# Hash attention with a gated MLP on one core: first-batch preparation in single steps, part of the later preparation moved into the first MLP layer, and a reordered start

## The chip, the cores and the metric

The kernel runs on one core of one Trainium2 chip. The metric is the device time of one execution in microseconds (us). A run on one core has no second core or die to be compared with, so runs are called slow only when they lie over 1.5% above the fastest of the same kernel. The profile's span is mostly some 1.8 us shorter than the device time of the same run.

In the profile's lines PE is TensorE's matmuls, PEld its weight loads, ACT is ScalarE, DVE VectorE, POOL GpSimd and SP SyncE; a q behind a name is that engine's instruction issue. A timeline line has the start and the length in us, the engine, the line of kernel.py, the operation, the tile written <- the tiles read, their sizes, a count, and in brackets the idle time before it and what ended that. A line of waits says who waited <- for whom: us in total, times, longest. Of the tiles, natq, natk and natv are loaded heads, n16x their 16-bit casts, blkq and blkk block transposes for the hash, projblk the projection, br the hash bits, qx and kx the extended queries and keys, and s_ps, av_ps and m_ps banks of PSUM.

## The reference, cut to what matters

```python
# q, k, v: (4, 8, 768, 64); proj: (64, 6)
q_bucket = sum over bits of ((q @ proj) > 0) * 2**bit        # 64 buckets
k_bucket = the same of k
scores = where(q_bucket == k_bucket, q @ k.T / 8, -1e9)
attn = softmax(scores)                                       # + 1e-9 in the denominator
x = (attn @ v) -> (3072, 512)
out = (h * cos(h)) @ w_out, h = x @ w_in                     # w_in 512x2048, w_out 2048x512
```

The kernel does the mask inside the score matmul: each query and key is extended by six rows of plus or minus a constant, its hash bits, so that a pair of unequal bits pushes the score far down before the exponential. Where no key matches, a uniform term of weight 1e-8 gives the mean of V.

## The kernel before

Heads are handled in pairs, two heads being 128 columns. Pair 0 to 15, four pairs for each of four batches. A *unit* is one key tile of one head: a score (two matmuls), one exponential of 128x768 on ACT, and, two units later, an AV tile of six matmuls. The preparation of a pair (casts on POOL, 32x32 block transposes on DVE, hash matmuls, bits, transposes of Q and K) is spread over the units of the pair before it. From the second batch on, every unit also takes one or two matmuls of the MLP's second layer of the batch before ("fill"); the first layer (L1, 16 pieces) stands in a block seven units into the next batch.

```python
    def hash_sums(pr, bank, cols, bh=None, t0=0):       # TensorE: 16 matmuls, four at a time
        nt = len(cols[0][2])
        hb = bank[:, 0:nt * 32]
        for c in range(2):
            for j, (w, hh, ts) in enumerate(cols):
                nc.tensor.matmul(out=hb[32 * j:32 * j + 32, :]..., lhsT=projblk[:, c]...,
                                 rhs=blk[pr][w][:, hh, ts[0]:ts[-1] + 1, c, :], ...)
        ...
    # ... cut: the start
        nc.scalar.dma_start(out=proj2, in_=proj.rearrange("(c p) i -> p c i", c=2))
        nc.sync.dma_start(out=nat[0][0][:, 0], in_=aps[0][:, 0])
        nc.scalar.dma_start(out=nat[0][1][:, 0], in_=aps[1][:, 0])
        ...
        warmup(8)                                       # matmuls of 512 columns on nothing
        for b_ in range(4):
            nc.vector.tensor_copy(
                out=projblk[32 * b_:32 * b_ + 32, :, b_, 0:NBITS], in_=proj2)
        blocks(0, 0)
    # ... cut: the preparation of the pairs, by unit
        for n in range(1, NP):
            s0 = 12 * (n - 1) - (0 if n < NEARLY else 4 if n == NEARLY else 6)
            if n < NEARLY:                              # pairs 1 to 4: transposes on TensorE
                at(s0 + 2, lambda n=n: load(n + 2, ...))
                at(s0 + o_, start)                      # casts, block transposes
                for half in range(2):
                    at(s0 + 3 + o_ + half, lambda ...: hash_a(half))
                at(s0 + 5 + o_, hash_b)
                ...
            else:                                       # pairs 5 to 15: transposes by DMA
                at(s0 - 1, lambda n=n: load(n + 1, nc.gpsimd))   # for 6 < n < 15
                at(s0, start)
                at(s0 + 2, hsh)                         # two DMA transposes into qx
                at(s0 + 3, hsh2)                        # hash, bits (DVE)
                at(s0 + 7, kc)                          # qx -> kx copies (DVE), bits by DMA
    # ... cut: the loop over units
            score(h, jt)
            pend.append((h, jt))
            for _ in range(2):
                if len(pend) > (4 if u < T else 2):
                    av_step()                           # the last tile of a head is followed by its norm (DVE)
            for f in acts.get(u, ()):
                f()
```

The softmax here doesn't subtract the row's maximum and nothing guards it: scores larger than these inputs give would overflow.

## Time and profile before

Median 310.24 us (310.15 to 310.26, three runs). The prediction shows the lines of this profile; in short:

| stage (us of the span) | length | what sets its pace |
|---|---|---|
| start, to the first exponential at 9.26 | 9.3 | loads, then one chain of hash, bits, transposes |
| first batch, to the first L1 matmul at 59.10 | 49.8 | ACT's 56 exponentials, with waits for scores |
| L1 of batch 0, rest of batch 1 and so on, to 263.2 | 204.1 | TensorE, 0.2 us idle in all |
| last MLP, to 308.4 | 45.2 | TensorE, then one copy and store |

The *pitch* of exponential n is its start minus that of exponential n-1 (there are 192; numbers are from 0); about 0.80 us when nothing is missing. "55 to 191" is the time from the start of the last exponential of the first batch to that of the last of all.

### The profile page before, as it was taken

What the parts mean: (1) busy time and instruction counts of PE and PEld (TensorE: products, weight loads), DVE (VectorE), ACT (ScalarE), POOL (GpSimd) and SP (SyncE); (2) the same over time, 40 slices, a digit from 0 to 9 for tenths busy, and PEclk for the clock granted to TensorE, in tenths of its full rate; (3) what the DMA queues carried; (4) which work ended last, traced back from release to release, by engine and by line L of the source; (5) the groups of instructions that cost most, each with busy time, mean ns of one, the idle gap of its engine ahead of it and who ended that gap; (6) DMA issues with size and microseconds to landing.
All of it is one profiled execution on the core that took longest, in us unless ns stands there. A gap on an engine that the chain in (4) does not pass through costs nothing.

```text
span 308.4 us, 7711 instructions
## 1 busy us (share of the span) xinstructions
PE 300.1 (97%) x3090; PEld 182.8 (59%) x3090; DVE 201.8 (65%) x434; ACT 234.3 (76%) x288; POOL 109.4 (35%) x180
## 2 busy tenths in 40 slices
PE   8899999899999999999999999999999999999995
PEld 3577677556566666555566666555566664565444
DVE  3665466877598988866777878766777343577211
ACT  3788999977899999766899999766899993577000
POOL 4898258378384684400064584100030000000000
PEclk9999999999999999999999999999999999999998
DMA  6969969289469856700169979200133223100121
GB/s 205 376 109 163 333 86 214 33 140 192 163 172 268 215 162 168 217 2 0 45 80 234 234 146 199 48 18 2 53 62 89 68 62 94 36 0 0 62 76 69
DMA packets 45332, 37.74 MB, mean 122 GB/s; under 512 B 32264, under 2 KB 39200, under 8 KB 45296
## 3 DMA queue, kind: packets, MB, share of 16 engines
q1 hardware_dynamic: 38080, 19.35, 28.9%
q0 software_dynamic: 6576, 17.17, 21.0%
q10 hardware_dynamic: 640, 0.72, 0.7%
q8 instruction: 24, 0.39, 0.5%
q14 instruction: 12, 0.10, 0.1%
HBM read 27.26 MB, written 6.29 MB: 109 GB/s over the span
## 4 chain that ended last, share of the span: by engine, by line
PE 89%; ACT 6%; DVE 3%; issue 1%; ACTq 0%; DVEq 0%
PE m_ps L370 26%; PE s_ps L320 18%; PE s_ps L252 18%; PE av_ps L278 10%; PE m_ps L320 6%; ACT pt L258 5%; PE m_ps L164 4%; PE av_ps L320 2%; PE s_ps L408 1%; PE m_ps L354 1%; PE m_ps L224 1%; DVE g L337 1%; DVE blkq L151 1%; ACT cos L332 1%; PE av_ps L164 1%
## 5 line engine op out<-in xcount | busy, mean ns | idle before, releaser
L258 ACT ACTIVATE pt<-s_ps,exp_bias 128x768 f16<-128x768 f32 x192 | 161.7, 899 | 11.1 <-PE s_ps L252 9.7
L370 PE MATMUL m_ps<-wout,g 128*128 128x512 f16 x368 | 105.6, 379 | 0.1
L252 PE MATMUL s_ps<-qx,kx 128*128 128x512 f16 (+1 forms) x384 | 93.8, 326 | 2.6 <-ACT pt L258 1.2
L278 PEld LDWEIGHTS <-pt 128*128 128x128 f16 x1152 | 58.7, 97 | 21.7
L320 PEld LDWEIGHTS <-win 128*128 128x128 f16 x512 | 50.0, 98 | 34.6 <-issue 0.2
L278 PE MATMUL av_ps<-vx,pt 128*128 128x65 f16 x1152 | 65.7, 193 | 0.0
L320 PE MATMUL s_ps<-xT,win 128*128 128x384 f16 x352 | 62.3, 326 | 0.1
L337 DVE TENSOR_TENSOR g<-s_ps,cos 128x768 f16<-128x768 f32 x44 | 42.1, 958 | 28.1 <-ACT cos L332 28.1
L332 ACT ACTIVATE cos<-s_ps,cos_bias 128x768 f16<-128x768 f32 x44 | 39.7, 901 | 26.8 <-PE s_ps L320 25.4
L252 PEld LDWEIGHTS <-kx 128*128 128x128 f16 x384 | 35.2, 97 | 31.1 <-issue 3.3
L138 POOL CAST vx<-natv 128x768 f16<-128x768 f32 x16 | 13.3, 829 | 92.8 <-PE av_ps L278 87.8
L370 PEld LDWEIGHTS <-g 128*128 128x128 f16 x368 | 31.2, 98 | 20.1 <-issue 3.3
L376 DVE COPY ob<-m_ps 128x512 f32<-128x512 f32 x23 | 15.8, 686 | 22.6 <-PE m_ps L370 22.6
L320 PE MATMUL m_ps<-xT,win 128*128 128x384 f16 x120 | 27.6, 326 | 0.0
L332 ACT ACTIVATE cos<-m_ps,cos_bias 128x384 f16<-128x384 f32 x30 | 16.3, 578 | 7.0 <-PE m_ps L320 7.0
L305 DVE TENSOR_TENSOR xn<-tot,rc 128x384 f16<-128x384 f32 x24 | 20.1, 839 | 0.8
L337 DVE TENSOR_TENSOR g<-m_ps,cos 128x384 f16<-128x384 f32 x30 | 15.7, 550 | 1.3 <-ACT cos L332 1.0
L300 DVE COPY dv<-av_ps 128x65 f32<-128x65 f32 x24 | 5.1, 211 | 16.9 <-PE av_ps L278 16.9
L140 POOL TENSOR_TENSOR vhalf<-natv 128x384 f32<-128x384 f32 x16 | 15.9, 996 | 0.0
L133 POOL CAST n16x<-natq 128x768 f16<-128x768 f32 (+1 forms) x16 | 13.1, 822 | 5.1 <-DMA natq<-in_q_dram 5.1
L133 POOL CAST n16x<-natk 128x768 f16<-128x768 f32 (+1 forms) x16 | 13.0, 813 | 5.5 <-DMA natk<-in_k_dram 5.5
L151 DVE STREAM_TRANSPOSE blkq<-natq 128x768 f32<-128x768 f32 x15 | 14.6, 975 | 0.3
(77 smaller groups left out, 274.8 us busy)
## 6 DMA issues: line engine op xcount, KB each, us to landing
out_dram<-ob SPq DMA_DIRECT2D x23, 256.0 KB
natq<-in_q_dram POOLq DMA_DIRECT2D x11, 384.0 KB, 3.9
natk<-in_k_dram POOLq DMA_DIRECT2D x11, 384.0 KB, 4.7
natv<-in_v_dram POOLq DMA_DIRECT2D x11, 384.0 KB, 5.7
win<-in_moe_w_in_dram POOLq DMA_DIRECT2D x4, 512.0 KB, 7.3
wout<-in_moe_w_out_dram POOLq DMA_DIRECT2D x16, 128.0 KB, 5.1
natq<-in_q_dram SPq DMA_DIRECT2D x4, 384.0 KB
natk<-in_k_dram SPq DMA_DIRECT2D x4, 384.0 KB
```

What stands on the lines that cost most here:

```text
L133: engs[w].tensor_copy(out=o_, in_=i_)
L140: nc.gpsimd.tensor_tensor(out=half, in0=nv[:, :, 0:3, :], in1=nv[:, :, 3:6, :], op=ALU.add)
L151: nc.vector.transpose(out=blk[pr][w].rearrange("p h t c r -> p (h t c r)"), in_=nat[pr][w].rearrange("p h f -> p (h f)"))
L252: nc.tensor.matmul(out=sp[:, c, 0:c1 - c0], lhsT=kx(pr)[:, hh, jt * P:(jt + 1) * P], rhs=qx(pr)[:, hh, c0:c1], start=True, stop=True)
L258: nc.scalar.activation(out=pt, in_=sp.rearrange("p c n -> p (c n)")[:, 0:S], func=ACTF.Exp, bias=exp_bias, scale=EXP_SCALE)
L278: nc.tensor.matmul(out=bank[:, qt * W:qt * W + D + 1], lhsT=pt[:, qt * P:(qt + 1) * P], rhs=vx_bufs[pr % 3][:, hh, jt, 0:D + 1], start=Fal ...
L305: nc.vector.tensor_tensor(out=dst, in0=tot[:, :, 0:D], in1=rc.unsqueeze(2).to_broadcast([P, T, D]), op=ALU.mult)
L320: nc.tensor.matmul(out=halves[c][:, 0:C2], lhsT=win_t[ft][:, ff * P:(ff + 1) * P], rhs=xT[(b, ft)][:, 3 * c:3 * c + 3, :], start=(ft == 0) ...
L332: nc.scalar.activation(out=c_, in_=h_, func=ACTF.Sin, bias=cos_bias, scale=1.0)
L337: nc.vector.tensor_tensor(out=g_, in0=h_, in1=c_, op=ALU.mult)
L370: nc.tensor.matmul(out=o_ps, lhsT=g[:, qt * P:(qt + 1) * P], rhs=wout_t[ff], start=(ff == 0), stop=(ff == NFF - 1))
L376: nc.vector.tensor_copy(out=ob, in_=o_ps)
```

## The change

Its intent, part by part:

- **Start.** The projection is written by four small transfers straight into its block form, behind the first operands' loads, and its four DVE copies go. The first score needs one K transpose instead of six. The warming matmuls read a constant instead of a tile that DVE zeroes first; the traces have them from 0.78 to 4.35 us instead of from 1.19 to 4.78.
- **First batch.** Each pair's hash is one step of 16 matmuls instead of two halves in two units; a table says in which unit each step stands; units with a heavy step (HEAVY) take fewer AV tiles. The uniform term of the first head moves to its third key tile.
- **Later pairs.** Loads go behind casts in POOL's queue, the k copies half a unit earlier (6.5 instead of 7), and pairs 9, 10, 13 and 14 are prepared in part inside the L1 blocks ("bits of pairs 9 and 13 inside L1").

```diff
+    SECOND = [0.5, 1.5, 3.5, 4.0]
+    PREP = {1: [0.5, 2, 4.5, 6, 7.5, 9, 9.5, 12, 14], 2: [14.5, 12, 12, 16, ...], 3: [22.5, 22, 24, 26, ...], 4: [...]}
+    HEAVY = set(int(x) for n in PREP for x in PREP[n][3:]) | set(int(x) for x in SECOND)
@@ av: the uniform term
-        if jt == 0 and h < DPE:
+        if jt == (2 if h == 0 else 0) and h < DPE:
@@ start
-        nc.scalar.dma_start(out=proj2, in_=proj.rearrange("(c p) i -> p c i", c=2))
         nc.sync.dma_start(out=nat[0][0][:, 0], in_=aps[0][:, 0])
         nc.scalar.dma_start(out=nat[0][1][:, 0], in_=aps[1][:, 0])
+        for b_, eng in enumerate((nc.scalar, nc.sync, nc.scalar, nc.sync)):
+            eng.dma_start(
+                out=projblk[32 * b_:32 * b_ + 32, :, b_, 0:NBITS],
+                in_=proj.rearrange("(c p) i -> p c i", c=2))
         warmup(8)
-        for b_ in range(4):
-            nc.vector.tensor_copy(
-                out=projblk[32 * b_:32 * b_ + 32, :, b_, 0:NBITS], in_=proj2)
@@ warmup
-                out=s_ps[1][:, 1, :], lhsT=wz[:, 0:P], rhs=wz, start=True, stop=True,
+                lhsT=nc.const_aps.tensor(1.0, [P, P], BF16),
+                rhs=nc.const_aps.tensor(1.0, [P, 512], BF16),
@@ pairs 1 to 4
-                for half in range(2):
-                    at(s0 + 3 + o_ + half, lambda hash_a=hash_a, half=half: hash_a(half))
+                def hash_a(n=n, held=held):
+                    held["bh"] = hash_sums(n, m_ps[1], [(j % 2, j // 2, range(T)) for j in range(4)])
+                units = PREP[n]
@@ pairs 5 to 15
-                at(s0 - 1, lambda n=n: load(n + 1, nc.gpsimd))          # s0 of before is 6 smaller
+            elif NEARLY + 1 < n < NP - 1 and n % 4 not in (1, 2):
+                at(s0 - 5, lambda n=n: load(n + 1, nc.gpsimd))
-                at(s0 + 7, kc)
+                units = LATE.get(n, [s0 - 6 + d_ for d_ in (0, 2, 3, 6.5)])
+            if n % 4 == 2 and n > NEARLY + 1:
+                # casts, DMA transposes and block transposes at L1's pieces 9 to 12
+                at(s0 - 4 + HS, hsh2)
+                at(s0 - 1.5, kc)
+                continue
+            if n % 4 == 1 and n > NEARLY:
+                in_l1[(n // 4 - 1, KL)] = [steps.pop()]                 # k copies and bits at L1's piece 3
@@ loop over units
+            for f in acts.get(u - 0.5, ()):
+                f()
+            if u >= 48:
+                avs = min(2, len(pend) - 2)
+            elif u in HEAVY:
+                avs = len(pend) - MAXP
+            else:
+                avs = min(2, len(pend) - (4 if u < T else LAG))
```

## The prediction

> **What bounds the kernel now.** I read the page first, then one table of windows cut at the borders of the stages (first exponential, first L1 matmul, start of the second L1, end of the attention, end), then the waits inside the first batch, then single timelines.
>
> ```profile
> PE 300.1 (97%) x3090; PEld 182.8 (59%) x3090; DVE 201.8 (65%) x434; ACT 234.3 (76%) x288; POOL 109.4 (35%) x180
> ...
> PE   8899999899999999999999999999999999999995
> ```
>
> PE is busy for 97%, but that is an average over stages, and busy counts overlapping drains. The windows, columns PE, PEld, DVE, ACT, POOL, clock, DMA share and GB/s, tell the stages apart:
>
> ```profile
> 0.00:9.26 9.26, 7.26 (x65) 3.01 (x66) 4.41 (x19) 2.88 (x6) 3.49 (x17) 1.00 0.73 232
> 9.26:59.10 49.84, 47.43 (x832) 34.20 (x833) 32.32 (x73) 45.96 (x56) 34.76 (x50) 1.00 0.85 191
> 59.10:125.30 66.20, 66.07 (x663) 40.31 (x663) 52.94 (x115) 58.52 (x72) 41.95 (x74) 1.00 0.76 178
> 125.30:263.20 137.90, 137.84 (x1296) 82.05 (x1294) 92.00 (x202) 111.75 (x136) 29.17 (x40) 1.00 0.39 90
> 263.20:308.40 45.20, 41.53 (x240) 23.28 (x238) 20.19 (x29) 15.19 (x21) 0.00 (x0) 0.98 0.11 42
> ```
>
> From 59.1 us on PE has no idle time to speak of: 0.13 us in the third row, 0.06 in the fourth, and in the last only the final copy and store. Whether PE also streams at its pace there is told by the chain that ended last: 80 matmuls of 512 columns in 17.27 us are 0.216 us each, so nothing lies between them. In the second row nobody is full: ACT, which has one 128x768 exponential per unit (a unit is one score tile, and 56 of them lie here), is busy 46.0 of 49.8 us. The waits in that window say for whom ACT stood still, and two timelines show the two sides of it:
>
> ```profile
> ACT pt L258 <- PE s_ps L252: 3.9, 9, 0.8
> ```
> ```profile
> 21.79 2.48 ACT L258 ACTIVATE pt<-s_ps,exp_bias 128x768 f16<-128x768 f32 x3
> 24.83 0.90 ACT L258 ACTIVATE pt<-s_ps,exp_bias 128x768 f16<-128x768 f32 x1 [0.55 <-PE s_ps L252]
> 25.91 1.77 ACT L258 ACTIVATE pt<-s_ps,exp_bias 128x768 f16<-128x768 f32 x2 [0.18 <-PE s_ps L252]
> ```
> ```profile
> 53.32 0.34 PE L278 MATMUL av_ps<-vx,pt 128*128 128x65 f16 x6
> ...
> 53.59 0.35 PE L164 MATMUL m_ps<-blkq,projblk 128*32 128x192 f32 x1
> ...
> 54.38 0.50 PE L252 MATMUL s_ps<-qx,kx 128*128 128x512 f16 x2
> ```
>
> The reader is to see that ACT waits for the score each time hash matmuls (L164) stand between two scores. Three exponentials without a wait take 2.48 us, and single ones start 0.78 to 0.84 us apart; I take 0.80. The start times of the first 56 run from 9.26 to 58.91, 49.65 us for 55 intervals, against 55 x 0.80 = 44.0.
>
> **What the Trainium skill says.** "TensorE: Matmul & The Clock Gate", section Back-to-back issue gap, gives N/2.4 + 2.5 ns, 216 ns for 512 columns; the 0.216 us above agrees, so after 59.1 us PE can't be made faster by order. The same page, Part 3, says that matmuls on different column tiles run concurrently; the trace agrees: four hash matmuls of 192 columns start within 20 ns (53.59 to 53.61), the next four 0.17 us later. So a hash of 16 matmuls is four such steps whatever it is cut into, and cutting it in two pays the change of kind twice. "Perfetto Trace Analysis", Optimization Strategy, says that a kernel can have several regimes and that one looks for gaps of the contended engine within each: here only the first 59 us have gaps. "DMA: Bandwidth & Descriptors", Issuing engines are not separate DMA queues: issuing from several engines only saves issue time; in the timeline each of the first loads costs its sequencer 0.41 to 0.46 us, and that is what the reordering of the first loads is worth.
>
> **The change, part by part.**
>
> *Order after unit 56.* I compared the orders of the two programs' PE instructions, scores as unit marks. From unit 56 (the first after the first L1) to the end they are the same, matmul for matmul. What moves there is DVE, POOL and DMA work: the transposes, casts and bits of pairs 9, 10, 13, 14 go into the L1 stages, and loads come behind casts. PE waits for none of these now, so this part is worth 0. Does it hurt? In L1 a DVE product waits for ACT by 0.3 to 1.0 us before nearly every piece, and a PSUM bank is refilled 0.65 to 1.3 us after its product ended (starts of L320 against ends of L337). A half transpose is 0.57 us (the 128x384 group), so it fits. I put 0, up to +0.3.
>
> *The start.* First exponential now at 9.26. The second operand's first half lands at 4.47 (its cast and its transpose both start then); its issue moves from 1.19 to 0.73 us, as the projection goes behind it, and the four projection copies (0.70 us of DVE) go. The transfers of the projection, now four, must land by about 4.5; before it landed at 3.08 with issue at 0.73, so with issue at 1.2 to 2.1 I expect 4.2. Gain 0.45. Then the first score needs one K transpose instead of six (five x 57 ns start to start = 0.28) and a short copy instead of 0.56 us, beside the Q copies: another 0.35. First exponential about 8.45: **-0.8 us**.
>
> *The 55 intervals.* What each preparation costs ACT now, from the exponentials' starts, as excess over 0.80 us: second head of pair 0, 0.61; pair 1, 1.59; pair 2, 1.24; pair 3, 1.15; pair 4, 0.84; pair 5, 0.55. Sum 5.98 (55 x 0.80 + 5.98 is 0.3 over 49.65, as many intervals are 0.78). Now the PE time of one unit's parts, from one start to the next kind's start: score 0.33, one AV tile 0.165, uniform term 0.165, six transposes 0.33, token bits 0.26, half hash 0.58 (0.47 and 0.11 of gap), whole hash 0.90 (53.48 to 54.38). Two halves are 1.16, so the single step saves 0.26 on PE, and more because no AV tile stands in its unit and only one unit is over. A score can be ready some 0.2 us early and no more, as two score banks alternate; so a unit loses its PE time minus 0.8 minus what of 0.2 was saved up. With the new order, unit by unit:
> - pair 0: the hash of the second head moves behind the second score, so the second exponential isn't held; the third is, by 0.35. Two transposes and an AV in unit 4: 1.155, loses 0.155.
> - pair 1: unit 6 has two AV tiles, the uniform term and the hash: 1.725, loses 0.725; the half transposes on DVE just before it come late, I guess 0.3 more; units 8 and 10 lose 0.135.
> - pairs 2, 3, 4: units 16, 26, 37 have score and hash alone, 1.23: lose 0.26, 0.42 (unit 25 had used up the slack), 0.23, and 0.03 twice.
> - pair 5 isn't changed: 0.55.
>
> Sum 3.2. The same rule on the old order gives 3.4 where the trace has 5.98, as it knows nothing of waits on DVE (a hash at 23.77 that waited for its transpose until 23.72). The new order puts transposes four and more units ahead of hashes, so I add only 0.2: 3.4. **-2.6 us**.
>
> Sum: 310.24 - 0.8 - 2.6 + 0 = **306.8 us**.
>
> **The rivals.**
> 1. *ACT becomes the bound of the first batch.* If smoothing the AV tiles works better than my rule, all waits but pair 5's go: 5.98 - 0.55 = 5.4, with the start 6.2, time 304.0. For it: the sum of the units' PE times in the new order is some 38 us of 44. Against: a unit with a whole hash is 1.23 us whatever stands around it.
> 2. *A transfer takes the place of the wait.* Pair 4's keys landed at 37.3 us (POOL waited 2.8 for them), with the DMA share at 1.0 from 24 to 42 us. The new order transposes pair 4 on DVE at units 33 and 34, about 35.5 us; if the keys still land at 37.3, DVE stands, the copies behind it and the hash of unit 37 come about 1 us late, time about 307.8 to 308.5. Against: their load stands behind the first pair's output transpose, whose input should be ready some 2 us sooner.
> 3. *The start gives nothing back*, as the projection's transfers, written as 24 byte pieces four times over, or the second head's keys (landed 7.5, behind two more issues now) come late: +0.8, time 307.6.
> 4. *DVE late in L1*: +0.3 to +1 in all, as above. The idle pieces speak against it.
>
> **Range and chances.** The most that can be had is 0.8 + 5.98 = 6.8, since nothing later can give. Over 2% needs 6.2 of these, nearly all. Rivals 2 to 4 together could eat the gain of the single step but hardly make the kernel slower, as the sum of PE work fell. Range 305.0 to 308.4; faster by over 2% 0.03, within 2% 0.965, slower 0.005.
>
> **What would show it.** First exponential near 8.45; start of the first L1 matmul near 55.7 instead of 59.10; from there to the end 249.3 us as before, within 0.3. In the first batch each pair has one wait of ACT for a score of 0.2 to 0.5 us where there were two, and pair 1 still the longest. ACT's waits for the score in that batch fall from 3.9 to about 2 us. I'd be wrong if the time from the first L1 to the end changed by over 0.5, if DVE stands for natk, or if ACT has no waits left in the first batch.

## The result, and the profile after

Median 310.20 us (309.95 to 310.42, three runs) against 310.24. The ratio is 0.9999 (95% interval 0.9977 to 1.0022): the same. Ratios here and below are the mean time of one kernel's fast runs over that of the other's of the same rounds, so not quite the ratio of the medians that are quoted. 306.8 was predicted, with a range of 305.0 to 308.4.

The same table of windows for the kernel after, cut at the same borders (columns as in the prediction):

```profile
0.00:9.69 9.69, 7.69 (x64) 3.36 (x64) 3.06 (x14) 2.78 (x5) 4.79 (x19) 1.00 0.75 220
9.69:58.45 48.76, 45.95 (x768) 31.84 (x768) 32.69 (x79) 45.54 (x56) 33.44 (x49) 1.00 0.78 196
58.45:124.76 66.31, 66.18 (x663) 40.33 (x663) 47.04 (x111) 58.51 (x72) 31.13 (x59) 1.00 0.68 140
124.76:263.93 139.17, 138.71 (x1296) 82.17 (x1294) 92.43 (x209) 111.80 (x136) 40.19 (x58) 1.00 0.41 107
263.93:308.60 44.67, 41.53 (x240) 23.25 (x238) 20.20 (x29) 15.17 (x21) 0.00 (x0) 1.00 0.11 42
```

The start is longer by 0.43 us, the first batch shorter by 1.08, the third row longer by 0.1 and the fourth by 1.27, where PE has 0.46 us idle instead of 0.06; the last row is shorter by 0.5. That isn't the change's doing: there the matmuls take 41.45 us from the start of the first to that of the last in both, and what follows, the last copy and store, 3.46 us instead of 3.96; over all 20 profiles it takes 3.44 to 4.73. (The granted clock of 0.98 before isn't the cause either, as its records fall to half at 306.9 us, behind the last matmul.) A gain in one stage stands against losses in two others.

**The start.** PE's timeline before, from the matmuls around the first bits to the transposes:

```profile
5.90 0.61 PE L408 MATMUL s_ps<-wz 128*128 128x512 f16 x1
...
6.69 0.39 PE L408 MATMUL s_ps<-wz 128*128 128x512 f16 x1
7.31 0.49 PE L224 MATMUL av_ps<-ident,n16x 128*128 128x128 f16 x6 [0.23 <-DVE n16x L203]
7.64 0.50 PE L224 MATMUL m_ps<-ident,n16x 128*128 128x128 f16 x6
```

The same after:

```profile
5.53 0.34 PE L175 MATMUL av_ps<-blkq,projblk 128*32 128x96 f32 x1 [1.19 <-DMA projblk<-in_proj_dram]
...
6.33 0.61 PE L420 MATMUL s_ps<-const-bfloat16-1.0 128*128 128x512 bf16 x1
...
7.14 0.61 PE L420 MATMUL s_ps<-const-bfloat16-1.0 128*128 128x512 bf16 x1
7.75 0.27 PE L235 MATMUL av_ps<-ident,n16x 128*128 128x128 f16 x1
7.81 0.85 PE L235 MATMUL m_ps<-ident,n16x 128*128 128x128 f16 x6
8.45 0.74 PE L235 MATMUL s_ps<-ident,n16x 128*128 128x128 f16 x5
```

The bracket says that the first hash matmul stood 1.19 us for the projection's transfers; both operands were transposed by 4.92. (The warming matmuls ended 0.43 us sooner than before, which is part of these 1.19; no run undoes that edit alone.) The last of the 16 hash matmuls starts at 6.03 instead of 5.60: that is the whole 0.43 us. And the warming matmul before the transposes takes 0.61 us where it took 0.39, and the twelve transposes 1.44 us (7.75 to 9.19) where they took 0.83 (7.31 to 8.14): PE runs at half its rate up to the first score. So the way from the last hash matmul to the first exponential is 3.66 us, as before, though less stands in it; where the rate is full, it is 3.02 (a1 below).

**The first batch.** ACT's waits for the score, which were to fall from 3.9 to about 2:

```profile
ACT pt L269 <- PE s_ps L263: 3.4, 7, 0.8
```

Summed by the pair that is being prepared, what the pitches have over 0.80 us (intervals over 0.02 only):

| being prepared | before | predicted | after |
|---|---|---|---|
| pair 0, second head | 0.61 | 0.5 | 0.70 |
| pair 1 | 1.59 | 1.3 | 1.27 |
| pair 2 | 1.24 | 0.3 | 0.49 |
| pair 3 | 1.15 | 0.5 | 1.23 |
| pair 4 | 0.84 | 0.3 | 0.65 |
| pair 5 | 0.55 | 0.55 | 0.55 |
| sum | 5.98 | 3.4 | 4.89 |

(The predicted values are rounded, and 0.135 is counted for each of units 8 and 10, so they add to 3.45.)

Pair 3 gained nothing. DVE's timeline shows for what its hash waits, PE's how long, and ACT's what follows:

```profile
30.46 0.57 DVE L166 STREAM_TRANSPOSE blkq<-natq 128x384 f32<-128x384 f32 x1
30.96 0.53 DVE L166 STREAM_TRANSPOSE blkk<-natk 128x384 f32<-128x384 f32 x1
31.42 0.52 DVE L246 COPY qx<-m_ps 128x768 f16<-128x768 f16 x1
31.86 0.56 DVE L166 STREAM_TRANSPOSE blkq<-natq 128x384 f32<-128x384 f32 x1
32.34 0.54 DVE L166 STREAM_TRANSPOSE blkk<-natk 128x384 f32<-128x384 f32 x1
```
```profile
32.76 0.35 PE L175 MATMUL m_ps<-blkq,projblk 128*32 128x192 f32 x1
...
32.93 0.35 PE L175 MATMUL m_ps<-blkk,projblk 128*32 128x192 f32 x1
```
```profile
34.30 0.90 ACT L269 ACTIVATE pt<-s_ps,exp_bias 128x768 f16<-128x768 f32 x1 [0.47 <-PE s_ps L263]
35.47 2.48 ACT L269 ACTIVATE pt<-s_ps,exp_bias 128x768 f16<-128x768 f32 x3 [0.27 <-PE m_ps L209]
```

DVE works without a gap from 29.99 on, and the last half transpose ends at 32.88. The hash starts at 32.76, and its fourth matmul, which needs that transpose, at 32.93: some 0.15 us. The second ACT line is another matter: its score was done, no engine is truly named, and yet it starts 0.27 us late. It comes back in the experiments.

**The later pairs.** DVE's timeline at the k copies of pair 12, before and after:

```profile
180.96 0.35 DVE L243 COPY kx<-qx 64x768 f16<-64x768 f16 x1 [0.38 <-DMA qx<-n16x]
...
182.60 0.98 DVE L151 STREAM_TRANSPOSE blkq<-natq 128x768 f32<-128x768 f32 x1
```
```profile
180.37 0.65 DVE L254 COPY kx<-qx 64x768 f16<-64x768 f16 x1 [3.86 <-DMA qx<-n16x]
...
183.65 0.97 DVE L162 STREAM_TRANSPOSE blkq<-natq 128x768 f32<-128x768 f32 x1
```

Before, the copies stood behind a norm, and when their turn came the DMA transpose was all but done. After, they stand ahead of it. DVE stands still for 3.86 us, the norm and the block transposes of pair 13 come 1.05 us later, and PE, which had a hash of those blocks ahead of the next score, waits. The waits of the second half, before and after:

```profile
DVE kx L243 <- DMA qx<-n16x: 0.7, 2, 0.4
```
```profile
DVE kx L254 <- DMA qx<-n16x: 5.8, 3, 3.9
PEld m_ps L175 <- DVE blkk L162: 0.7, 1, 0.7
PE m_ps L175 <- DVE blkk L162: 0.3, 1, 0.3
```

The pitch of exponential 142 grows from 1.61 to 2.59 us. The shares of the chain that ended last say the same from afar, before and then after: DMA is in it now.

```profile
PE 89%; ACT 6%; DVE 3%; issue 1%; ACTq 0%; DVEq 0%
```
```profile
PE 84%; ACT 7%; DMA 3%; DVE 3%; issue 2%; ACTq 0%; DVEq 0%
```

### The profile page after: what moved, and what is told of

Read it like the earlier page. It is cut to its first block, busy times and chain, and to the rows that moved or that the text cites. A ratio compares the mean times of both kernels' runs of the same rounds, so it can differ in the third digit from the quotient of the medians.

```text
span 308.6 us, 7602 instructions
## 1 busy us (share of the span) xinstructions
PE 300.1 (97%) x3026; PEld 180.9 (59%) x3026; DVE 195.4 (63%) x438; ACT 233.8 (76%) x288; POOL 109.6 (35%) x184
## 4 chain that ended last, share of the span: by engine, by line
PE 84%; ACT 7%; DMA 3%; DVE 3%; issue 2%; ACTq 0%; DVEq 0%
PE m_ps L382 24%; PE s_ps L332 18%; PE s_ps L263 17%; PE av_ps L289 9%; ACT pt L269 6%; PE m_ps L332 6%; PE m_ps L175 4%; DMA qx<-n16x 2%; PE av_ps L332 2%; DMA projblk<-in_proj_dram 1%; PE m_ps L366 1%; PE m_ps L235 1%; DVE g L349 1%; ACT cos L344 1%; PE av_ps L175 0%
## 5 line engine op out<-in xcount | busy, mean ns | idle before, releaser
L289 PEld LDWEIGHTS <-pt 128*128 128x128 f16 x1152 | 56.9, 97 | 19.5
L289 PE MATMUL av_ps<-vx,pt 128*128 128x65 f16 x1152 | 64.0, 193 | 0.0
L593 POOL COPY mark<-g 128x1 f16<-128x1 f16 x4 | 0.8, 190 | 50.4 <-DVE g L349 50.4
L254 DVE COPY kx<-qx 64x768 f16<-64x768 f16 x22 | 10.7, 517 | 8.8 <-DMA qx<-n16x 8.6
L317 DVE TENSOR_TENSOR xn<-tot,rc 128x384 f16<-128x384 f32 x24 | 15.4, 643 | 0.8
```

The lines of the kernel that those rows point to most:

```text
L289: nc.tensor.matmul(out=bank[:, qt * W:qt * W + D + 1], lhsT=pt[:, qt * P:(qt + 1) * P], rhs=vx_bufs[pr % 3][:, hh, jt, 0:D + 1], start=(h ...
L317: nc.vector.tensor_tensor(out=dst, in0=tot[:, :, 0:D], in1=rc.unsqueeze(2).to_broadcast([P, T, D]), op=ALU.mult)
```

## The experiments

My theory after the first look: three separate faults eat the gain, namely the projection's small transfers, the place of the k copies, and DVE's order at pair 3. The rivals: the moves into L1 do the harm; the first batch just can't be had faster; a chance of these single runs. All variants are edits of the changed kernel; all gave correct results. "Median" is over the runs of the label; each call ran on a chip of its own, with the kernel before at 309.93 to 310.23 in all five.

### First call: one part undone at a time

**a1_proj_old**: the projection is loaded as before.

```diff
+        nc.scalar.dma_start(out=proj2, in_=proj.rearrange("(c p) i -> p c i", c=2))   # first of all
-        for b_, eng in enumerate((nc.scalar, nc.sync, nc.scalar, nc.sync)): ...       # the four transfers
+        for b_ in range(4): nc.vector.tensor_copy(out=projblk[...], in_=proj2)
```

> The changed kernel with the projection loaded as before: one transfer ahead of all others, then four copies on DVE; all else of the change kept. Theory (the four small transfers land late, at about 5.5 us, and PE, left without work for 1.2 us, then runs its next matmuls slowly): the first hash starts near 5.05 instead of 5.53, the transposes after it take about 0.5 us instead of 1.1, the first exponential comes at 8.7 to 8.9 instead of 9.69, and the time falls by 0.5 to 1.0 us against the changed kernel. Rival (the new order of the transposes and copies delays the first score by itself): the first exponential stays above 9.3 and the time stays within 0.3 us of the changed kernel.

Measured: 308.73 us (307.56 to 309.89, four runs), ratio 0.9954 (0.9912 to 0.9996). In its profile the hash starts at 4.55, the transposes take 0.83 us and the first exponential is at 8.40 instead of 9.69. Of these 1.29 us, 0.66 are the hash, whose last matmul starts at 5.37 instead of 6.03, and 0.64 the way from there at full rate (3.02 instead of 3.66). So the projection's transfers were a fault, and the shorter way to the first score gives what was predicted where the rate is full; that the rate is full here isn't shown to be this edit's doing (see g2). The late wait of DVE for pair 12 is still there, 2.2 us long, but short enough that exponential 142 has its 1.62. Two things were not expected. Exponentials 28, 76, 124 and 172 lost the delay that the changed kernel has there. And the runs scatter by 2.3 us.

**a2_bits_behind**: the k copies and bits behind the AV tile and norm again.

```diff
-                units = LATE.get(n, [s0 - 6 + d_ for d_ in (0, 2, 3, 6.5)])
+                units = LATE.get(n, [s0 - 6 + d_ for d_ in (0, 2, 3, 7)])
```

> The changed kernel with one number altered: the copies of K and the bits of the later pairs stand behind the AV steps of their unit again, not ahead of them. Theory (DVE, which works in order, stands 3.9 us for the transposed Q of pair 12, the division of a head stands behind it, so pair 13's block transposes and with them its hash come 1 us late): the interval of exponential 142 falls from 2.59 to 1.6 us, the others stay, time 0.9 to 1.0 us below the changed kernel. Rival (the transfers are late whatever stands where, as loads were moved): the interval stays above 2.2 us.

Measured: 310.58 us (308.29 to 311.89), ratio 1.0006 (0.9955 to 1.0056). The profile does what it should: no wait of DVE for the transposes, exponential 142 at 1.62, 55 to 191 in 196.25 us instead of 197.21. Yet the median doesn't show it, as this kernel's start came out worse in the profiled run (first exponential 10.06) and its runs scatter by 3.6 us. The mechanism is shown in the trace, its worth in the median is not, in these four runs.

**a3_late_old**: pairs 7 to 15 prepared wholly as in the kernel before.

```diff
-            elif NEARLY + 1 < n < NP - 1 and n % 4 not in (1, 2):
-                at(s0 - 5, ...)
+            elif NEARLY + 1 < n < NP - 1:
+                at(s0 - 7, ...)
+   k copies at 7; the parts for n % 4 == 1 and 2 and the loads inside L1 taken out
```

> The changed kernel with everything for pairs 7 to 15 scheduled as before (nothing of the preparation inside the L1 stages, loads where they were). If moving work into L1 is worth nothing to PE, as predicted, the stretch from the first L1 matmul to the end is that of the kernel before, and the time is that of the run with the bits behind, within 0.3 us, about 309.2. If the moves into L1 are worth something that the wait at exponential 142 hides, it is slower than the run with the bits behind by over 0.4 us.

Measured: 311.16 us (310.01 to 312.32), ratio 1.0032 (1.0000 to 1.0065). Exponential 142 is well, but a new stall of PE of 1.0 us stands at 117 us, before a score of pair 8, and 55 to 191 is 197.54. Undoing the late part doesn't bring the late time back.

**a4_blk3_early**: the half transposes of pair 3 four units earlier.

```diff
-    PREP = {... 3: [22.5, 22, 24, 26, ...
+    PREP = {... 3: [22.5, 18, 19.5, 26, ...
```

> The changed kernel with the DVE block transposes of pair 3 at units 18 and 19.5 instead of 22 and 24, ahead of pair 2's row copies. Theory (the hash of unit 26 waits for a DVE chain of copies and transposes that is full from 30.0 to 32.9 us): the interval of exponential 27 falls from 1.37 to about 1.2 and that of 28 from 1.17 to about 0.85, time 0.4 to 0.5 us below the changed kernel. Rival (the single hash with two AV tiles and the uniform term around it is what costs, PE time alone): both intervals stay within 0.1.

Measured: 311.59 us (310.90 to 314.27), ratio 1.0072 (1.0018 to 1.0125). Pitch 27 fell from 1.37 to 1.22, pitch 28 stayed 1.17: DVE's order was worth 0.15, the rest is something else. Here the projection happened to land in time, and the first exponential is at 8.34: the start that was predicted, with the very code that gave 9.69. The time is worse because exponential 142 is at 3.54, with DVE waits for the transposed operand of 3.85 and 0.90 us. Kernels with the changed kernel's order at this place have 1.62 (a1), 2.59 (the changed kernel), 3.03 (g2) and 3.54 (a4, e5) in their profiles: the late order doesn't lose a fixed amount.

### Second call: faults removed together, and two costs by themselves

**c0_base**: a1 and a2 together. **c1_smooth**: c0, a4's table and AV tiles dealt out by hand around the heavy units.

```diff
+            avs = {4: 0, 5: 2, 6: 0, 7: 2, 8: 1, 49: 0}.get(u, avs)
             for _ in range(avs):
```

> Two of the single edits together: the projection loaded as before, and the copies of K and the bits of the later pairs behind the AV steps. If the start and the DVE wait in front of pair 13 are what took the gain away, the first exponential is at 8.4 to 8.9, the interval of exponential 142 is 1.6, the stretch from exponential 55 to 191 is 195.8 to 196.0 us as in the kernel before, and the time is 2.0 to 2.6 us (0.65 to 0.85%) below the kernel before, with less scatter than the changed kernel. If something else holds it, it stays within 1 us of the kernel before.

> As the run of the two edits together, with the first batch smoothed further: pair 3's block transposes at units 18 and 19.5, no AV tile in units 4, 6 and 49 (the double transposes and the hashes of pairs 1 and 5), two in units 5 and 7, one in unit 8. By the unit sums of the prediction this takes 0.16 from exponential 5, 0.7 from exponential 7, 0.15 from 27 and 0.16 from 50: about 1.2 us below the run of the two edits together, 306.0 to 306.8 us. If ACT is held by something other than PE's work per unit, less than 0.5 us.

Measured: c0 308.27 us (307.56 to 309.76, six runs), ratio 0.9944 (0.9920 to 0.9969); c1 307.91 (307.40 to 309.56), ratio 0.9933 (0.9910 to 0.9956). With both faults mended the change is a gain. c1's AV tiles were to give 1.2 us and gave 0.4, not told apart from nothing: exponential 7 stayed at 1.71, because before it the hash of pair 1 still waits for the copies and block transposes of DVE, and not for AV tiles.

**c2_two_step**: c0 with the hashes of pairs 1 to 4 in two halves again.

```diff
-                steps += [hash_a, hash_b]
+                steps += [lambda f=hash_a: f(0), lambda f=hash_a: f(1), hash_b]     # three tiles each, in two units
```

> As the run of the two edits together, with the hashes of pairs 1 to 4 cut into halves in two following units again. If the single step is what the first batch gains by (0.26 us of PE time a pair, and one AV tile fewer in the way), exponential 55 comes 0.8 to 1.6 us later after exponential 0 than in that run. If the gain is only in the moved AV tiles, within 0.3 us.

Measured: 317.22 us (316.51 to 319.47), ratio 1.0218 (1.0189 to 1.0247). From the first exponential to number 55 it took 49.99 us against 48.06 in c0: the single step is worth 1.9 us (d1, with the same edit, has 50.06), more than I had put on it. (The edit also counts the second half's unit as heavy.) The surprise is the other 9 us, all in the third batch: exponential 142 has a pitch of 9.25. The waits of that stage:

```profile
DVE kx L255 <- DMA qx<-n16x: 10.4, 3, 7.6
PEld m_ps L176 <- DVE blkq L163: 6.3, 2, 5.6
```

SyncE's two DMA transposes of pair 12 took 5.35 us where c0's took 2.98, and POOL issued the load of pair 13 in the same microsecond (174.49 to 176.66 against 175.25); in c0 that load was issued at 168.16 to 170.30, well ahead. Nothing in the edit touches this stage but the time at which it is reached. PE then stands 5.53 us for the hash of pair 13, and the clock records have half rate from 190.0 to 196.8, so part of the loss follows from the wait.

**e5_act_plus1**: the changed kernel, with one more instruction on ACT at the start and nothing else.

```diff
+        for _ in range(2):
             nc.scalar.activation(out=warm, in_=exp_bias, func=ACTF.Exp, bias=0.0, scale=1.0)
```

> The changed kernel with the warming exponential of the start issued twice, so that every later ACT instruction stands one place further on. In the four traces with one more transfer issued by ACT, exponentials 28, 76, 124 and 172 started 0.2 to 0.3 us after both their semaphore and ACT were ready; in those with one fewer none of these did; the late ones stand at places 63, 191, 319 and 447 of ACT's instructions. If the place is the cause, the intervals of 28 (1.17) and of 76, 124 and 172 (1.00) fall to about 0.86 and 0.80 though there is more to do, worth some 0.5 us. If they come from the kernel's work, they stay.

Measured: 308.58 us (308.31 to 311.13), ratio 0.9966 (0.9932 to 0.9999). The profiled run is the slowest, with pitches of 2.58 and 3.54 at exponentials 94 and 142, where DVE waits for transposed operands. The delayed exponentials in ACT's timeline of the changed kernel (the line at 35.47 shown above) became one unbroken run of four here:

```profile
32.81 3.34 ACT L269 ACTIVATE pt<-s_ps,exp_bias 128x768 f16<-128x768 f32 x4 [0.46 <-PE s_ps L263]
```

Pitches 76, 124 and 172 are 0.80 instead of 1.00. More work, and the delay is gone: it depends on the place of an instruction in ACT's stream. In the trace the four delayed exponentials are instructions 63, 191, 319 and 447 of ACT (from 0, issues of transfers included), 128 apart. All six profiles that keep the four projection transfers and add nothing to ACT show the delays (the changed kernel, a2, a3, a4 and, below, f3 and g2); none of the others does. They cost 0.31 and three times 0.15 us, 0.76 in all (three times 0.15 and not 0.20, as the exponentials behind make some good). The Trainium skill, "Perfetto Trace Analysis", section The 4-stage abstract model, says that an instruction has 64 bytes; the profile's instruction queue with packets of 8 KB then brings 128 at a time (an estimate: 8,192 over 64). That the delay stands where one such block ends is likely, and not shown. The trace speaks against a wait for the transfer itself: the packets nearest to exponentials 76, 124 and 172 of the changed kernel start at 101.0, 170.4 and 240.7 us, 0.8 to 1.1 us after them (it doesn't say for which engine they are).

### Third call: why c2 lost 9 us, and what three parts are worth

**d1_two_load**: c2 with the loads two units earlier, as in the kernel before. **d2_smooth_load**: c1 with the same edit.

```diff
-                at(s0 - 5, lambda n=n: load(n + 1, nc.gpsimd))
+                at(s0 - 7, lambda n=n: load(n + 1, nc.gpsimd))
```

> The two-step kernel with one edit more: the loads of the pairs 9, 12 and 13 are issued two units earlier, ahead of the casts, as in the kernel before. The two-step kernel lost some 9 us in the third batch (exponentials 130 and 142, pitch 3.05 and 9.25 us), where DVE waited 2.6 and 7.6 us for the transposed pairs 11 and 12. Theory L (the load of pair 13, issued behind late casts, met the DMA transposes of pair 12): with the early loads the loss goes, exponential 142 under 2.0 us pitch, time 309.5 to 310.5 against 317.2, as the first batch still pays the 1.9 us of the two steps. Rival (whole halves of hashes upset something else there, or it was one odd run of transposes): exponential 142 stays above 5 us and the time above 315.

> The best version so far (307.91) with the loads two units earlier, as in the kernel before. If late loads cost it anything in the fast runs, the time from exponential 55 to 191 falls from 195.8 to about 195.3 and the run to run range of 2.2 us narrows to under 1.5; time 307.2 to 307.7. Rival (its copies never wait for the transposes, so the loads are hidden either way): 307.9 within 0.3, same range.

Measured: d1 311.55 us (310.86 to 313.72), ratio 1.0054 (1.0024 to 1.0085); exponential 142 at 1.62. What is left of the wait, in the same view:

```profile
DVE kx L255 <- DMA qx<-n16x: 2.9, 2, 2.2
```

So the late load was the cause of most of it: the two kernels differ in nothing else, and the pitch at that place is that of the kernel before again. It is not all, since pair 11's copies still wait 2.2 us (exponential 130 at 3.33; in c2 and d1 alike pair 12's load is issued 1.2 us ahead of pair 11's transposes), which is why the 309.5 to 310.5 was missed. d2: 307.73 us (307.17 to 308.69), ratio 0.9922 (0.9903 to 0.9942), no wait for transposes or bits left in its later batches; against c1 nothing can be told apart, so where the copies don't wait, the loads are hidden either way.

**d3_smooth_uni0**: c1 with the uniform term of the first head back at its first key tile.

```diff
-        if jt == (2 if h == 0 else 0) and h < DPE:
+        if jt == 0 and h < DPE:
```

> The best version so far (307.91) with the uniform term of the first head back at its first key tile. Theory (the term is one wide matmul of 0.165 us, moved within a stretch where ACT waits for the hash and not for AV): no change, 307.9 within 0.3, first exponential the same within the scatter of the start. Rival (at the first tile it waits for the sums of V on POOL and holds PE): the exponentials 4 to 7 come 0.3 to 1.5 us later, time 308.2 to 309.4.

Measured: 309.15 us (308.50 to 310.91), ratio 0.9970 (0.9947 to 0.9994). The rival was right. Its waits between 10 and 15.5 us have a line that c1's don't:

```profile
PE av_ps L279 <- POOL vs L155: 0.9, 1, 0.9
```

The term needs the sums of V, which POOL makes from a load that lands late. With the start sooner, PE would stand 0.9 us for them; two key tiles later they are ready. The part that looked like a detail is worth 0.9 us here. The other 1.1 us of its profiled run is one stall, at a score of pair 11:

```profile
175.19 0.38 PE L383 MATMUL m_ps<-wout,g 128*128 128x512 f16 x1
176.66 0.50 PE L264 MATMUL s_ps<-qx,kx 128*128 128x512 f16 x2 [1.09 <-DMA kx<-br]
```

The score waits for the key bits, which SyncE writes by small transfers behind the k copies. With that, the stall of a3 (1.0 us, pair 8) and one of c0 (0.7, pair 11) have a name: their waits show the same releaser.

**d4_smooth_lateold**: c1 with pairs 7 to 15 as before (a3's edit).

> The best version so far (307.91) with the pairs 7 to 15 prepared wholly as in the kernel before: no bits or transposes inside L1. Theory (with the k copies behind the AV steps the move into L1 is worth nothing, as PE waits for none of it): 307.9 within 0.4, exponentials 55 to 191 in 195.6 to 196.0. Rival (the move takes a real wait away): 308.3 to 309.0, with waits of PE for blkq or blkk in batches 2 and 3 that the best version lacks.

Measured: 309.46 us (308.57 to 311.22), ratio 0.9967 (0.9948 to 0.9986). The rival was right again, with another wait than the one it named: PE stands three times for key bits, 1.3 us at most, and 55 to 191 is 197.96 instead of 195.79. So the late part of the change, "bits inside L1", removes a real wait: 2.2 us in these two profiles, and 1.4 us by the ratios, where d2 has 0.9922. In the profile of before that wait was 0.2 us.

### Fourth and fifth call: the bits, the projection and the rate at the start

What was open here: why single kernels of nearly the same late order lose 0.7 to 1.4 us at one place, and which part of the start costs.

**f1_kbits_early**: d2, with the key bits written right behind the hash; only the query bits, whose rows the transposes overwrite, stay behind the k copies. **f3_after_kbits**: the changed kernel with this and with a2's edit.

```diff
                 def hsh2(n=n):
                     hash_mm(n, m_ps[1 - state["m"]])
+                    bits_dma(n, (1, 3))
 ...
-                    bits_dma(n, (0, 1, 2, 3))
+                    bits_dma(n, (0, 2))
```

> The version with smooth AV tiles and early loads (307.73, runs 307.17 to 308.69), with the key bits of the pairs 5 to 15 written right behind their hash; only the query bits stay behind the k copies, as only their rows are overwritten by the transposes. Theory (the single stalls of 0.7 to 1.4 us in a3, c0, d3, d4 are scores that wait for the last bits to land, kx bits in the trace): no PE wait for kx bits or qx bits is left in the batches 2 to 4 in the profiled run, time 307.2 to 307.7, and the range of the six runs falls under 1.2 us. Rival (the bits' transfers are in time and something else holds PE): range and median as d2, 307.7 within 0.3. Rival 2 (the early bits stand in SyncE's queue ahead of transposes and hold those): waits of DVE or PE for DMA qx or xT appear, time over 308.

> The changed kernel with the k copies behind the AV steps (as in a2, 310.58, runs 308.29 to 311.89) and the key bits behind the hash. Theory: time from exponential 55 to 191 is 195.7 to 196.3 (195.84 plus the 0.45 of the three late exponential stalls, if those show), no PE wait for bits, time 309.0 to 309.6. Rival (as for f1): as a2, 310 to 311.

Measured: f1 308.67 us (308.06 to 309.65), ratio 0.9963 (0.9945 to 0.9980); no wait for bits, but the first L1 grew by 0.86 us (exponential 55 to 56: 24.47 instead of 23.61). Its waits there:

```profile
PE s_ps L333 <- DMA xT<-xn: 0.7, 1, 0.7
```

The early bits of pair 5 stand in SyncE's queue ahead of the last output transpose, which the first L1 needs. Rival 2 of that expectation, for one pair. f3: 309.38 us (three fast runs, 309.14 to 309.66; a fourth, 314.81, was slow), ratio 0.9979 (0.9962 to 0.9996); 55 to 191 in 196.23, no wait for bits. That is 0.39 over the kernel before, and the three delayed exponentials on ACT are 0.45: the late loss of the changed kernel is accounted for by its two causes.

**f2_proj_behind**: f1 with the projection's one transfer behind the second operand's load instead of ahead.

```diff
-        nc.scalar.dma_start(out=proj2, in_=proj.rearrange("(c p) i -> p c i", c=2))
         nc.sync.dma_start(out=nat[0][0][:, 0], in_=aps[0][:, 0])
         nc.scalar.dma_start(out=nat[0][1][:, 0], in_=aps[1][:, 0])
+        nc.scalar.dma_start(out=proj2, in_=proj.rearrange("(c p) i -> p c i", c=2))
```

> f1_kbits_early with the projection's one transfer issued behind the second operand's on ScalarE's queue instead of ahead. Theory (the reordering itself is worth the 0.45 us that the prediction gave it; it was the four small transfers that failed): natk lands at 4.0 instead of 4.4 to 5.3, first exponential 8.2 to 8.5, time 0.3 to 0.7 under f1. Rival (the projection lands late behind the loads, whatever its form): hash waits for projblk, first exponential 8.8 or later, time equal to f1 or above.

Measured: 310.64 us (309.79 to 311.68), ratio 1.0025 (1.0011 to 1.0039). The rival was right. The projection's copies could start at 4.40 instead of 3.21, and the first exponential is at 10.86 instead of 9.69. So the order itself is wrong, and not only the four pieces: the projection is 1.5 KB, it is wanted first, and behind two loads of 192 KB it comes 1.2 us later, with DVE's block transposes behind its copies.

**g1_warm10**: d2 with ten warming matmuls instead of eight. **g2_after_warm11**: the changed kernel with eleven. **g3_warm_kbits**: g1 with key bits early for pairs 6 to 15 only.

```diff
-        warmup(8)
+        warmup(10)        # g2: 11
```

> d2_smooth_load (307.73; runs in two groups, 307.17 to 307.32 and 308.15 to 308.69) with ten warming matmuls at the start instead of eight. Theory (the half rate in some runs comes from TensorE's idle pieces between 4.35 us and the hash): matmuls after the hash take 390 ns in the profiled run, the first exponential is at 8.6 to 9.0, all six runs lie within 0.7 us, median 307.1 to 307.5. Rival (the rate is set by chance in each run whatever stands there, or one more gap at 4.9 to 5.5 is enough): two groups as before, median 307.5 to 308.3; then the two added matmuls at half rate delay the first hash to 5.2 and cost up to 0.3.

> The changed kernel with eleven warming matmuls instead of eight, which last to 5.6 us at half rate, when its projection lands. Theory (its late projection costs twice, the wait and then the half rate): warm matmuls after the hash 390 ns instead of 607, the twelve transposes 0.83 us instead of 1.44, first exponential at 8.6 to 8.9 instead of 9.69, time 309.0 to 309.7 against 310.2. Rival (the half rate has nothing to do with the wait): 607 ns again, first exponential 9.7 to 10.0, time 310.2 to 310.6.

> g1_warm10 with the key bits of the pairs 6 to 15, not of pair 5, right behind the hash. Theory: the first L1 is as in d2 (exponential 55 to 56 23.61 us, not 24.47 as in f1), no wait for bits or transposes in the batches 2 to 4, exponentials 55 to 191 in 195.8, time as g1 within 0.3 and never over 308.5. Rival (early bits stand ahead of transposes for pair 6 or later too): DVE or PE waits for DMA qx or xT, 308 and above.

Measured: g2 309.32 us (308.32 to 311.15, four runs), ratio 0.9982 (0.9956 to 1.0008). In its profile the hash starts at 5.56, as late as in the changed kernel, and PE is at its full rate:

```profile
6.10 0.39 PE L420 MATMUL s_ps<-const-bfloat16-1.0 128*128 128x512 bf16 x1
```

The transposes take 0.83 us and the first exponential is at 8.97 instead of 9.69 (0.07 over what was expected): 0.11 of that by the hash, 0.61 by the rate. Whether the longer warming did it is open. Of the 16 other profiles with eight warming matmuls of the new kind, 9 have the full rate at the transposes and 7 half, and the idle time before the hash doesn't tell them apart: 1.45 us in a3, 0.75 in e5 and 0.49 in a4 went with the full rate, 0.25 in d2 and 0.22 in f1 with half. Three profiles of three at full rate with more warming (g1, g2, g3) can be chance. g2's profiled run is the slowest of its four for other reasons: exponential 142 has 3.03, and from the start of the last matmul to the end it takes 4.68 us. g1: 308.02 us (307.59 to 308.34, five runs), ratio 0.9931 (0.9918 to 0.9943). First exponential 8.40, spread 0.75 instead of d2's 1.52, but the median isn't lower. In its profiled run the time from the start of the last matmul to the end is 4.73 us, where d2 and c1 have 3.61: the last store, too, varies by a microsecond. g3: 308.02 us (307.40 to 308.91), ratio 0.9933 (0.9919 to 0.9947); its first L1 is as in d2 (23.60), 55 to 191 is 195.78, as expected, but one run was over 308.5, so the start isn't all of the scatter.

The versions c1, d2, g1 and g3 lie at 307.73 to 308.02 and can't be told apart; all four are below the kernel before, and their intervals don't reach the changed kernel's. d2 has the lowest ratio: 0.78% under before (0.58 to 0.97%).

## Why the prediction was wrong

**First exponential 8.45 (-0.8): failed, +0.43.** Of its two halves, the shorter way through one K transpose and a short copy was right, and worth more than its 0.35: from the last hash matmul to the first exponential it takes 3.02 us at full rate, 3.66 before. The failing step is "The transfers of the projection, now four, must land by about 4.5 ... I expect 4.2". The hash started at 5.53, and at 4.76 to 5.80 in other profiles of the same start. f2 shows that a single transfer in the second place gives 4.40, so 4.2 was an estimate for one transfer and not for four. Rival 3 had said it; it was believed too little. The 0.45 wasn't there anyway: with the keys' load issued sooner, both operands were transposed by 4.92 instead of 5.05, as the keys' transpose stands behind that of the queries on DVE, which starts at 3.88. Where the four transfers landed in time, the last hash matmul starts at 5.32 (a4) and 5.39 (e5), against 5.60 before. And one term wasn't in the sum at all: PE can stay at half its rate up to the first score, which makes the way from the last hash matmul 3.66 to 3.94 us (seven profiles) instead of 3.02 to 3.26 (the other twelve of the new start). How the start falls out in one profile is partly luck: the same code gave 9.69, and 8.34 in a4.

**First batch -2.6: the mechanism right, the size off; -1.08 in the profile.** That PE's time between two scores sets the pitch, and that the single step shortens it, held: it is worth 1.9 us for four pairs (c2 against c0). Pairs 1 and 5 came out as predicted (pair 1 with a guess of 0.3 for DVE). The mis-sized term is what a unit loses, "minus what of 0.2 was saved up". Exponential 17, behind pair 2's hash, has 0.42 over 0.80 where 0.26 was put, with no wait for DVE: nothing was saved up. Exponentials 26, 31, 36 and 46 have 0.11, 0.18, 0.15 and 0.18 where nothing was put: between their scores and those before stand six transposes and two more AV-sized pieces, without a pause of PE (40.56 to 41.58 us for one of them). That is 0.8 of the 1.5 us that are missing. ACT's delay of exponential 28 is 0.31. DVE's order at pair 3 is 0.15 (a4), so "so I add only 0.2" for waits on DVE was not far off. The last 0.2 stands at pair 0: exponential 2 has 1.23, where the profiles at full rate have 1.02 but others at half rate 0.95 to 1.11, so its cause is open.

**After unit 56, 0 up to +0.3: failed, +1.38 from exponential 55 to 191.** The step that failed is "PE waits for none of these now, so this part is worth 0", drawn from the same PE order. The order on PE was the same, but that on DVE and in the transfers was not: k copies ahead of the norm cost 0.97 at one place (a2, f3), ACT's delayed exponentials 0.45. The other half of the sentence was wrong too, to the other side: the moves into L1 do save a wait, of the score for key bits, which shows as 0.2 us in the profile of before and as 1 to 2 us when the old late order is put under the new first batch (a3, d4). Why it is larger there than in the kernel before isn't settled.

**What it cites.** The section that it names for 216 ns calls that the gap of a single matmul and gives about 131 ns for a stream of 512-column matmuls; no stretch here shows that, and the trace's 0.216 us decides.

**Rivals.** ACT as the bound: no, its waits are still 3.4 us. Pair 4's keys in place of the wait: pair 4 has 0.65 instead of 0.84, so no. DVE late: yes, but not where it was looked for, in L1's products; it was at the k copies.

**The signs.** The first was missed, the second (first L1 at 55.7) was 58.45, and the third was over its limit: from the first L1 to the end it took 250.15 instead of 249.3 us, of which the last store hides 0.5. Each missed sign named its stage rightly: with start and late order mended, c1 has 8.84, 56.92 and 248.93.

Without the two faults the change does gain: c0, at 308.27, and c1 and d2, at 307.7 to 307.9 with further edits, lie inside the range, if 1 to 1.5 us over 306.8. That there was something to gain in the first 59 us held; what was missing above all was the cost of each new place in a queue.

The half rate needs a word. The Trainium skill, "TensorE: Matmul & The Clock Gate", section Part 1 (The HAM clock gate), says that TensorE starts at half its clock, changes after about 3.4 us of sustained work, and that the point varies from run to run as the window runs freely. The trace agrees: the warming matmuls of all profiles are 0.43 us apart, twice the 0.216 us of later ones. The full rate is there with the hash, at 4.5 to 5.8 us, in eight profiles, first seen between 5.7 and 7.3 us in six (the kernel before among them) and only with the first score or behind it, at 9.1 to 10.4 us, in six; d4 has it at 4.5 us and, by its clock records, half of it again from 7.5 to 10.9. c1 and d2, with equal starts and the same gap behind the warming, have first exponentials at 8.84 and 9.85. So between equal starts a microsecond is chance, as far as these traces tell. That this splits d2's six runs into 307.17 to 307.32 and 308.15 to 308.69 is likely; only one run of each kernel has a profile, so it isn't shown.

## What to carry to other kernels

Comparing the order on the busiest engine isn't enough: for each moved instruction ask what it waits for, and what stands behind it in its own in-order queue; an instruction that waits for a transfer goes behind the work that doesn't. The smallest transfer that everything needs goes first and in one piece. A start in one profile is taken apart, hash here and rate there, before an edit is credited with it. And where a wait is just hidden, as the bits and loads are here, a change elsewhere can bring it out, so a part that is worth nothing in one profile may be worth a microsecond in the next.

## What the Trainium skill lacked or had wrong

- "TensorE: Matmul & The Clock Gate", Part 1, calls the penalty of the clock's ramp under 1% of a typical kernel and advises not to fit to a count of slow matmuls. Here half rate costs the first exponential 0.4 to 0.9 us of 310 (3.66 to 3.94 us behind the hash instead of 3.02 to 3.26), within that 1%, but as large as the effects under study. Whether more warming gets it back isn't shown.
- "Runtime: NRT & Kernel Launch", Instruction fetch mechanics, has instructions come in blocks of 16 KiB, 256 of them, and the crossing of a block mostly hidden. Here one instruction queue has packets of 16,384 bytes and the other of 8,192; on ACT the instructions 63, 191, 319 and 447, 128 apart, started 0.2 to 0.3 us late in six profiles, and not when one instruction more stood ahead of them; 0.76 us in all.
- "DMA: Bandwidth & Descriptors" has no time for a small transfer behind larger ones: 1.5 KB usable at 3.06 to 3.25 us when issued first, 4.40 when issued behind two loads of 192 KB, and the hash waited until 4.76 to 5.80 for four of them.
- The same page gives a rate for DMA transposes, not how their time grows beside loads: two of them held SyncE for 2.98 us with the next load long issued and for 5.35 us with it issued in the same microsecond, and what needed them waited up to 7.6 us. Nearness alone doesn't settle it: pair 11's two, with a load issued 1.2 to 2.5 us ahead, took 2.79 to 4.01 us.
